# Parallel sum of a spectral filter and a spatial-shift MLP on one core: who normalises the first group, who splits w1's first quarter, and who takes one block's statistics

## The chip, the cores and the metric

The kernel runs on one core of a Trainium2 chip. The metric is the device time of one execution in microseconds. The engines are named as in the profile: PE (TensorE matmuls), PEld (TensorE weight loads), DVE (VectorE), ACT (ScalarE), POOL (GpSimd), SP (the engine that issues the transfers).

## The reference

With xn the layer norm of x (2048 tokens of 448 channels), the output is x + A(xn) + B(xn):

```python
# A: spectral filter
X = rfft2(xn) * (w_r + 1j * w_i);  a = irfft2(X)
# B: spatial-shift MLP
h  = gelu(layernorm(xn) @ w1)                    # 448 x 448
hs = shifted_quarters(h, (+1, -1, +2, -2)) @ w2  # 448 x 448
x1 = xn + hs
b  = x1 + gelu(layernorm(x1) @ w3) @ w4          # 448 x 1792, 1792 x 448
out = x + a + b
```

## The kernel before

The 2048 tokens are 16 blocks of 128, held as eight tiles `xt` of two blocks each. Four groups of four blocks are in `GRP`: group 0 is blocks 14, 15, 0, 1 and group 1 is blocks 2, 3, 4, 5. Every fp32 matrix product is made of three fp16 products: each operand is split into a high part (its fp16 rounding) and a low part (what is left), and high*high, high*low and low*high are added up in PSUM.

The change lies in the first 20 us, up to the first two groups' product with w1. The work there goes through these steps:

1. **Statistics and normalisation** (`norm1`, `stats`). For each block of a group DVE runs a statistics instruction (L306) and an aggregate (L307). Five short DVE instructions (L324 to L328) make scale and bias for the four blocks at once; then each block is scaled in place by the engine that the list `apply` names (L336 on DVE or POOL, L333 on ACT). `norm1` returns a function, `refine`, that adds ten small POOL instructions (L343 to L352) which sharpen the inverse root; their last result, `gsc`, is first wanted by the GELU.
2. **The scale of w1** (`squares`, `powers`). ACT adds up the squares of w1, DVE reduces them (L258), PE adds over the partitions with a matmul of ones into `pm` (L260), and DVE makes powers of two from that (L262 to L267): `s1`, the factor for w1, is written by L266.
3. **The split of w1** (`split_w`), in four row quarters t = 0 to 3. For t = 0 and 1 ACT writes the high part with the scale in it (L280) and DVE the low part (L281). For t = 2 and 3 POOL first scales the quarter in place (L276), ACT copies it to fp16 (L277), and POOL subtracts (L278).
4. **The transposition of x** (`T1`, `transpose_split`). For each of four column pieces PE transposes the group's four blocks (L389), ACT writes the high part (L393) and DVE the low part (L394). The fourth piece holds high and low part in one tile.
5. **The product with w1** (`w1_in`, L420), 11 matmuls for a block. For group 0 the first 24 run through quarters 0 and 1 for all four blocks, then quarters 2 and 3 follow for two of the blocks, 34 matmuls in all. Then PE transposes group 1, `T1(1)`, whose first transposition reads block 2.

Each engine works through its own list in order and waits at the head of it for semaphores. The order within a list is set by a scheduler that goes by priority and its own estimates, and by `behind(key)`, which lets an instruction be listed only after those recorded under that key; `pins` passes such keys to the statistics of `norm1`. ACT's outputs that nobody reads (the squares) go to a scratch tile, `xr`.

Of the kernel before, what the change touches and what calls it, by code (L numbers as in the profile page):

```python
# [125 lines left out]
def body(tc, nc, x, wf, w1, w2, w3, w4, c_g, c_n, c_small, out):  # L126
    V, A, P, T, SY = nc.vector, nc.scalar, nc.gpsimd, nc.tensor, nc.sync
# [31 lines left out]
    pc = pool("pc")  # L159
# [8 lines left out]
    def xb(b):  # L168
        return xt[b // 2][:, b % 2]
# [11 lines left out]
    xr = pw.tile([128, 904], F32, name="xr")  # L181
# [22 lines left out]
    w1s = stage("w1s", F, 0).rearrange("p (t n) -> p t n", t=4)  # L204
# [66 lines left out]
    def absmax(out_, in_):  # L271
        V.tensor_reduce(out=out_, in_=in_, axis=AX.X, op=ALU.max, apply_absolute_value=True)

    def split_w(hi, lo, src, s, low=None):
        if low is P:
            after["ps"] = (P.tensor_scalar(out=src, in0=src, scalar1=s, scalar2=0.0, op0=ALU.mult, op1=ALU.add).ins,)  # L276
            i = A.activation(out=hi, in_=src, func=AF.Copy)  # L277
            j = P.tensor_tensor(out=lo, in0=src, in1=hi, op=ALU.subtract)  # L278
            return i.ins, j.ins
        i = A.activation(out=hi, in_=src, func=AF.Copy, scale=s)  # L280
        j = V.scalar_tensor_tensor(out=lo, in0=src, scalar=s, in1=hi, op0=ALU.mult, op1=ALU.subtract)  # L281
        return i.ins, j.ins

# [13 lines left out]
        V.tensor_tensor(out=q, in0=q, in1=a, op=ALU.mult)  # L297
        V.scalar_tensor_tensor(out=r, in0=q, scalar=1.5 * 0.375, in1=w, op0=ALU.add, op1=ALU.mult)

    def stats(src, key, mv=None, pins=None):  # L300
        if mv is None:
            mv = pc.tile([128, 4, 2], F32, tag="mv", bufs=3, name=f"mv{key}")
        for i, s in enumerate(src):
            st = pc.tile([128, 6], F32, tag="st", bufs=4, name=f"st{key}_{i}")
            with behind(*pins[i]) if pins else contextlib.nullcontext():
                V.bn_stats(out=st, in_=s)  # L306
            V.bn_aggr(out=mv[:, i, :], in_=st)  # L307
        return mv
# [7 lines left out]
    vy = vyi.bitcast(F32)  # L316
    nma, nm1 = (pc.tile([128, NB], F32, name=f"nm{t}") for t in "a1")

    def norm1(g, apply, pins=None):

        bs, c = GRP[g], slice(4 * g, 4 * g + 4)
        mv, a, y, nm = mva[:, c], va[:, :, c], vy[:, :, c], nma[:, c]
        stats([xb(b) for b in bs], f"a{g}", mv, pins)
        V.tensor_scalar(out=a[:, 1], in0=mv[:, :, 1], scalar1=1.0 + EPS, scalar2=EPS * EPS, op0=ALU.mult, op1=ALU.add)  # L324
# [3 lines left out]
        i = V.scalar_tensor_tensor(out=nm, in0=mv[:, :, 0], scalar=-1.0, in1=y[:, 1], op0=ALU.mult, op1=ALU.mult)  # L328
        after["c", g] = (i.ins,)
        for k, b in enumerate(bs):  # L330
            y_, m_ = y[:, 1, k:k + 1], nm[:, k:k + 1]
            if apply[k] is A:
                i = A.activation(out=xb(b), in_=xb(b), func=AF.Identity, scale=y_, bias=m_)  # L333
                after["na", g] = (i.ins,)
            else:
                i = apply[k].tensor_scalar(out=xb(b), in0=xb(b), scalar1=y_, scalar2=m_, op0=ALU.mult, op1=ALU.add)  # L336
                after["n" if apply[k] is V else "np", g] = (i.ins,)

        q, z = (pc.tile([128, 2, 4], F32, tag=f"v{t}", bufs=2, name=f"v{t}{g}") for t in "qz")
        w, r = vw[:, :, c], vr[:, :, c]  # L340

        def refine():
            P.tensor_tensor(out=q, in0=y, in1=y, op=ALU.mult)  # L343
            P.tensor_tensor(out=q, in0=q, in1=a, op=ALU.mult)
# [3 lines left out]
            P.tensor_tensor(out=z, in0=w, in1=w, op=ALU.mult)  # L348
            P.tensor_tensor(out=z, in0=z, in1=q, op=ALU.mult)
            P.tensor_scalar(out=z, in0=z, scalar1=-0.5 * 0.375 ** 3, scalar2=1.5 * 0.375, op0=ALU.mult, op1=ALU.add)  # L350
            P.tensor_tensor(out=r, in0=z, in1=w, op=ALU.mult)
# [55 lines left out]
    w1p = p1.tile([128, 8, D], F16, name="w1p")  # L407
# [6 lines left out]
    def w1_in(g, units, ts, passes=range(3)):  # L414
        for p in passes:
            for t in ts:
                for i, pm in units:
                    wi, xi = ((0, 0), (0, 4), (4, 0))[p]
                    if t < 3 or p != 1:
                        m = T.matmul(pm[:, :D], xTs[g][:, xi + t, 128 * i:128 * i + 128], w1p[:, wi + t],  # L420
                                     start=t == 0 and p == 0, stop=t == 3 and p == 2)
        after["u"] = (m.ins,)
# [450 lines left out]
    for t in range(3):  # L873
        squares(m1[:, t:t + 1], w1s[:, t])
    squares(m1[:64, 3:4], w1s[:64, 3])
    n1 = [norm1(0, [P,V,P,V])]
    with behind("n", 0):
        s1, r1 = powers(m1, 4, "1", "mm")
    first = [bank("mm" if k < 2 else "sp", f"pw1_0{k}") for k in range(4)]
    for t in range(4):  # L880
        with behind("p1"):
            T1(0, [t])
        with behind("a0", t):
            after["w1", t] = split_w(w1p[:, t], w1p[:, 4 + t], w1s[:, t], s1, P if t > 1 else V)
# [12 lines left out]
    T1(1)  # L897
    with behind("T", "a1"):
        for unit in list(enumerate(first))[n:2]:
            w1_in(0, [unit], [2, 3])  # L900
    with behind("n", 1), behind("u"):
        s2, r2 = powers(m2, 1, "2", first[0][:, 448:512])
    with behind("p2"):
        for unit in list(enumerate(first))[2:]:
            w1_in(0, [unit], [2, 3])
# [31 lines left out]
    with behind("a2"):  # L937
        n1 = [norm1(3, [P, P, P, P])]
# [120 lines left out]
    for n in range(17):  # L1059
# [4 lines left out]
        if n:  # L1064
            b = bs[n - 1]
# [42 lines left out]
```

## Time and profile before

| what | value |
|---|---|
| median of 3 runs | 408.12 us (407.88 to 408.28) |
| the profiled execution's own time | 408.05 us |
| its span in the trace | 406.3 us |
| PE busy | 399.9 us, 98% of the span |
| DVE, ACT, POOL busy | 333.6 us (82%), 255.1 us (63%), 100.4 us (25%) |
| granted TensorE clock | 0.998 |

The profiled execution took 1.75 us more than its span, which is what lies before the first and behind the last instruction of the trace. In the profile's rows the first two numbers are the start of the row, in microseconds from the span's start, and its length; "x2" is the number of instructions in the row; the brackets give the idle time of the engine before it and what ended it.

### The profile page before, as it was taken

How to read it: one execution, taken by the hardware profiler on the slowest of the kernel's cores; microseconds unless marked ns; L12 is line 12 of the kernel's file. 1: busy time of each engine (PE TensorE's matmuls, PEld its weight loads, DVE VectorE, ACT ScalarE, POOL GpSimd, SP SyncE). 2: the span in 40 equal slices, each digit the busy share in tenths (PEclk: the TensorE clock that was granted, in tenths of full speed). 3: DMA queues.
4: the chain of work that ended last, by engine and by line, in shares of the span. 5: the costliest groups of instructions: out<-in, count | busy, mean ns of one | idle time of the engine just before them, and what ended most of it. 6: DMA issues, size and time to landing. Idle time of an engine off the chain costs nothing.

```text
span 406.3 us, 8732 instructions
## 1 busy us (share of the span) xinstructions
PE 399.9 (98%) x3391; PEld 297.2 (73%) x3391; DVE 333.6 (82%) x702; ACT 255.1 (63%) x433; POOL 100.4 (25%) x158
## 2 busy tenths in 40 slices
PE   8999999999999999999999999999999999999996
PEld 3555555865667877777878878777677779998995
DVE  5898799898947887988698888965999999965645
ACT  4788889874568857655698878853354544353431
POOL 6859910111146946500021111110000000000000
PEclk9999999999999999999999999999999999999999
DMA  8978975567489661637256556510011023100101
GB/s 280 389 272 160 249 152 138 122 121 163 95 225 266 234 191 46 219 95 185 72 144 164 162 142 161 139 27 2 24 69 70 24 90 92 47 2 2 45 2 45
DMA packets 54596, 52.07 MB, mean 128 GB/s; under 512 B 35678, under 2 KB 48542, under 8 KB 54556
## 3 DMA queue, kind: packets, MB, share of 16 engines
q1 hardware_dynamic: 54556, 51.53, 46.0%
q8 instruction: 26, 0.43, 0.4%
q14 instruction: 14, 0.11, 0.1%
HBM read 38.28 MB, written 3.67 MB: 103 GB/s over the span
## 4 chain that ended last, share of the span: by engine, by line
PE 87%; POOL 5%; DMA 2%; DVE 2%; ACT 2%; issue 1%; SPq 0%; POOLq 0%; ACTq 0%
PE pw L400 33%; PE acc L808 23%; PE pw L478 6%; PE side L778 4%; PE acc L778 3%; PE pu L667 3%; PE ps L567 3%; PE pe L688 2%; PE pp L622 2%; PE px L639 2%; PE py L709 2%; PE pw L420 2%; DMA w1s<-w 1%; POOL xt L336 1%; DMA h<-x2mem 1%
## 5 line engine op out<-in xcount | busy, mean ns | idle before, releaser
L400 PE MATMUL pw<-x2mem,w3p 128*128 128x256 f16 x1232 | 151.3, 273 | 0.0
L400 PEld LDWEIGHTS <-w3p 128*128 128x128 f16 x1232 | 118.9, 98 | 19.3
L808 PE MATMUL acc<-w4p,hf 128*128 128x448 f16 (+1 forms) x516 | 104.4, 348 | 0.0
L808 PEld LDWEIGHTS <-hf 128*128 128x128 f16 x516 | 50.1, 98 | 37.6
L726 ACT ACTIVATE pw<-pw,pe 128x512 f32<-128x512 f32 x42 | 27.4, 654 | 26.8 <-PE pw L400 26.6
L729 DVE SCALAR_TENSOR_TENSOR hf<-pw,h,hf 128x512 f16<-128x512 f32 x42 | 31.3, 746 | 12.9 <-ACT hf L728 12.7
L478 PE MATMUL pw<-w2p,h 128*128 128x448 f16 x176 | 35.8, 353 | 0.9 <-DMA h<-x2mem 0.9
L420 PE MATMUL pw<-w1p,xT 128*128 128x448 f16 x176 | 34.9, 352 | 0.1
L648 POOL TENSOR_TENSOR z<-te 128x450 f32<-128x450 f32 x16 | 15.7, 983 | 70.8 <-DVE te L646 65.9
L728 ACT ACTIVATE hf<-pw,h 128x512 f16<-128x512 f32 x42 | 28.9, 687 | 5.0 <-PE acc L808 4.0
L478 PEld LDWEIGHTS <-h 128*128 128x128 f16 x176 | 17.0, 98 | 17.0 <-DMA h<-x2mem 2.0
L744 ACT ACTIVATE hz<-g,h 128x896 f16<-128x896 f32 x14 | 14.6, 1044 | 23.1 <-DVE g L741 23.1
L420 PEld LDWEIGHTS <-xT 128*128 128x128 f16 x176 | 17.1, 99 | 16.1 <-DVE xT L394 0.4
L778 PEld LDWEIGHTS <-hz 128*128 128x128 f16 x294 | 28.3, 98 | 0.6
L629 ACT ACTIVATE pf<-pp 64x450 f16<-64x450 f32 x32 | 17.4, 544 | 12.5 <-DVE pf L630 9.7
L630 DVE TENSOR_TENSOR pf<-pp,pf 64x450 f16<-64x450 f32 x32 | 19.9, 622 | 5.1 <-ACT pf L629 4.7
L745 DVE SCALAR_TENSOR_TENSOR hz<-g,h,hz 128x896 f16<-128x896 f32 x14 | 16.1, 1148 | 6.8 <-ACT hz L744 6.8
L550 POOL TENSOR_TENSOR f<-xr 128x452 f32<-128x452 f32 x16 | 19.7, 1251 | 0.6
L558 DVE TENSOR_TENSOR xh<-f,xh 128x452 f16<-128x452 f32 x16 | 14.3, 916 | 5.7 <-ACT xh L557 5.7
L644 ACT ACTIVATE te<-px 64x450 f32<-64x450 f32 x32 | 17.3, 541 | 1.2 <-PE px L639 0.6
L738 ACT ACTIVATE g<-pw,pe 128x512 f32<-128x512 f32 x14 | 9.6, 683 | 11.3 <-PE pw L400 11.3
L547 POOL TENSOR_TENSOR xr<-xf 128x452 f32<-128x452 f32 x8 | 9.2, 1156 | 22.3 <-issue 16.4
(188 smaller groups left out, 705.7 us busy)
## 6 DMA issues: line engine op xcount, KB each, us to landing
wc<-wf SPq DMA_DIRECT2D x32, 225.0 KB, 3.7
wl<-wf SPq DMA_DIRECT2D x8, 450.0 KB, 4.3
xt<-x SPq DMA_DIRECT2D x8, 448.0 KB, 7.1
xf<-x SPq DMA_DIRECT2D x8, 448.0 KB, 4.6
loads<-x SPq DMA_DIRECT2D x7, 448.0 KB, 4.0
out<-xt SPq DMA_DIRECT2D x13, 224.0 KB, 1.9
w3raw<-w SPq DMA_DIRECT2D x3, 896.0 KB, 10.8
gn<-c_g SPq DMA_DIRECT2D x16, 128.0 KB, 3.0
```

Source lines behind the costliest of these rows:

```text
L400: T.matmul(ps_out, wp[:, wi + t, cols], xT[:, xi + t, tok], start=t == 0 and wi + xi == 0, stop=t == 3 and wi == 4)
L420: m = T.matmul(pm[:, :D], xTs[g][:, xi + t, 128 * i:128 * i + 128], w1p[:, wi + t], start=t == 0 and p == 0, stop=t == 3 and p == 2)
L478: T.matmul(pm[:, :D], h[:, k], w2p[:, w], start=n == 0, stop=n == 10)
L550: P.tensor_tensor(out=f[:, :, k:k + 2].rearrange("p b s d -> p s b d"), in0=u[:, :, 0], in1=u[:, :, 1], op=op)
L629: A.activation(out=hi, in_=src, func=AF.Copy)
L630: V.tensor_tensor(out=lo, in0=src, in1=hi, op=ALU.subtract)
L644: A.activation(out=e[64 * h:64 * h + 64], in_=px_[64 - 64 * h:128 - 64 * h, :2 * DF], func=AF.Copy)
L726: A.activation(out=pm, in_=pm, func=AF.Gelu_apprx_tanh, scale=r3)
L728: i = A.activation(out=h[:, 0], in_=pm, func=AF.Copy, scale=h3)
L729: j = V.scalar_tensor_tensor(out=h[:, 1], in0=pm, scalar=h3, in1=h[:, 0], op0=ALU.mult, op1=ALU.subtract)
L778: m = T.matmul(to, h[:, hi, 128 * blk:128 * blk + 128], b[wi], start=new and n == 0, stop=n == 2 and (last if blk in (2, 5, 3, 0) else end ...
L808: m = T.matmul(to, h[:, hi, o:o + 128], w4p[0][:, wi, f, r], start=first and f % 2 == 0 and n == 0, stop=end and f % 2 == 1 and n == 2, sk ...
```

## The change

Three things are moved, all in the steps above, and the two places in the text that follow from them.

- Group 0: the list of normalising engines goes from P, V, P, V to P, V, V, V. Block 0 moves from POOL to DVE.
- w1, quarter 0: `split_w` has a new argument `high`. For t = 0 POOL writes the scaled high part straight to fp16, in place of ACT; DVE still makes the low part.
- Group 1: `stats` has a new argument `on_a`. For block 5 ACT makes mean and variance with two activations that accumulate (the mean of x, then the squares of mean minus x) and a third that scales the sum; the DVE statistics and aggregate of that block go. The keys behind which the other three blocks' statistics are listed change, and the squares of w2 on ACT are listed behind the new third activation.

The matmuls of the last two blocks of group 0 with quarters 2 and 3 are now two pieces of text with the same key; a loop over nothing is gone.

```diff
-    def split_w(hi, lo, src, s, low=None):
+    def split_w(hi, lo, src, s, low=None, high=None):
         if low is P:
...
-        i = A.activation(out=hi, in_=src, func=AF.Copy, scale=s)
+        if high is P:
+            i = P.tensor_scalar(out=hi, in0=src, scalar1=s, scalar2=0.0, op0=ALU.mult, op1=ALU.add)
+        else:
+            i = A.activation(out=hi, in_=src, func=AF.Copy, scale=s)
         j = V.scalar_tensor_tensor(out=lo, in0=src, scalar=s, in1=hi, op0=ALU.mult, op1=ALU.subtract)
...
-    def stats(src, key, mv=None, pins=None):
+    def stats(src, key, mv=None, pins=None, on_a=None):
...
         for i, s in enumerate(src):
+            if i == on_a:
+
+                sq = pc.tile([128, 1], F32, tag="sq", bufs=2, name=f"sq{key}")
+                junk = xr.bitcast(F32)[:, :D]
+                with behind(*pins[i]):
+                    A.activation(out=junk, in_=s, func=AF.Copy, scale=1.0 / D, accum_out=mv[:, i, 0:1])
+                A.activation(out=junk, in_=s, func=AF.Square, scale=-1.0, bias=mv[:, i, 0:1], accum_out=sq)
+                u = A.activation(out=mv[:, i, 1:2], in_=sq, func=AF.Copy, scale=1.0 / D)
+                after["sq"] = (u.ins,)
+                continue
...
-    def norm1(g, apply, pins=None):
+    def norm1(g, apply, pins=None, on_a=None):
...
-    n1 = [norm1(0, [P,V,P,V])]
+    n1 = [norm1(0, [P, V, V, V])]
...
-            after["w1", t] = split_w(w1p[:, t], w1p[:, 4 + t], w1s[:, t], s1, P if t > 1 else V)
+            after["w1", t] = split_w(w1p[:, t], w1p[:, 4 + t], w1s[:, t], s1, (V, V, P, P)[t], P if t in (0,) else A)
...
-    n = 2
-    for unit in list(enumerate(first))[:n]:
-        w1_in(0, [unit], [2, 3])
+    units = list(enumerate(first))
+    w1_in(0, [units[0]], [2, 3])
+    w1_in(0, [units[1]], [2, 3])
...
-    n1.append(norm1(1, [P, V, A, V], [("r1",), ("a0", 0), ("w1", 0), ("w1", 1)]))
-    with behind("w1", 3):
+    n1.append(norm1(1, [P, V, A, V], [("e1",), ("w1", 0), ("w1", 1), ("a0", 3)], 3))
+    with behind("sq"):
         squares(m2, flat(w2s))
...
     with behind("p2"):
-        for unit in list(enumerate(first))[2:]:
-            w1_in(0, [unit], [2, 3])
+        w1_in(0, [units[2]], [2, 3])
+    with behind("p2"):
+        w1_in(0, [units[3]], [2, 3])
```

Lines from L281 on move down by 3 in the changed kernel, and those from L319 on by 13 (L336 becomes L349, L343 becomes L356).

The first place is DVE's list from the end of group 0's normalisation to w1's scale. `xt_83` holds blocks 14 and 15, `xt_76` blocks 0 and 1, `xt_77` blocks 2 and 3; `pt` and `pe` are the scale's small tiles. Before:

```order
L336 TENSOR_SCALAR xt_83<-xt_83,vy,nma 128x448
L336 TENSOR_SCALAR xt_76<-xt_76,vy,nma 128x448
L258 TENSOR_REDUCE pt_200<-m_167 128x1
L306 BN_STATS sta_0_298<-xt_77 128x6
L307 BN_AGGR mva<-sta_0_298 128x2
L262 TENSOR_SCALAR pt_200<-pm_202 128x1
L264 TENSOR_SCALAR pe_205<-pt_200 128x1
L266 TENSOR_SCALAR pe_205<-pe_205 128x1
```

And now:

```order
L349 TENSOR_SCALAR xt_83<-xt_83,vy,nma 128x448
L349 TENSOR_SCALAR xt_76<-xt_76,vy,nma 128x448 x2
L258 TENSOR_REDUCE pt_200<-m_167 128x1
L262 TENSOR_SCALAR pt_200<-pm_202 128x1
L264 TENSOR_SCALAR pe_205<-pt_200 128x1
L266 TENSOR_SCALAR pe_205<-pe_205 128x1
L267 TENSOR_SCALAR pe_205<-pe_205 128x1
L319 BN_STATS sta_0_298<-xt_77 128x6
```

One more normalisation stands ahead of L258, and block 2's statistics have moved from between L258 and L262 to behind the powers of two.

The second place is POOL's list from the normalisation of group 0 to that of group 1. `w1s` is w1 as loaded, `w1p` its split; `vq`, `vw`, `vz`, `vr` and `gsc` are the small tiles of `refine`. Before, from the second of its two normalisations of group 0:

```order
L336 TENSOR_SCALAR xt_76<-xt_76,vy,nma 128x448
L276 TENSOR_SCALAR w1s<-w1s,pe_205 128x448 x2
...
L348 TENSOR_TENSOR vz_199<-vw 128x8
L349 TENSOR_TENSOR vz_199<-vz_199,vq_198 128x8
L278 TENSOR_TENSOR w1p<-w1s,w1p 128x448
L350 TENSOR_SCALAR vz_199<-vz_199 128x8
L278 TENSOR_TENSOR w1p<-w1s,w1p 128x448
L351 TENSOR_TENSOR vr<-vz_199,vw 128x2x4
L352 TENSOR_SCALAR gsc<-vr,pe_205 128x4
L343 TENSOR_TENSOR vq_319<-vy 128x8
L336 TENSOR_SCALAR xt_77<-xt_77,vy,nma 128x448
```

And now:

```order
L281 TENSOR_SCALAR w1p<-w1s,pe_205 128x448
L276 TENSOR_SCALAR w1s<-w1s,pe_205 128x448 x2
...
L361 TENSOR_TENSOR vz_199<-vw 128x8
L278 TENSOR_TENSOR w1p<-w1s,w1p 128x448
L362 TENSOR_TENSOR vz_199<-vz_199,vq_198 128x8
L278 TENSOR_TENSOR w1p<-w1s,w1p 128x448
L363 TENSOR_SCALAR vz_199<-vz_199 128x8
L364 TENSOR_TENSOR vr<-vz_199,vw 128x2x4
L365 TENSOR_SCALAR gsc<-vr,pe_205 128x4
L356 TENSOR_TENSOR vq_320<-vy 128x8
L349 TENSOR_SCALAR xt_77<-xt_77,vy,nma 128x448
```

The high part of quarter 0 (L281) stands where block 0's normalisation stood, but it needs `s1`, which that did not; the two subtractions L278 stand one small step earlier each; and group 1's block 2 still comes last.

More of the change, by code (lines that the diff above doesn't have):

```diff
@@ L317, in body @@
     nma, nm1 = (pc.tile([128, NB], F32, name=f"nm{t}") for t in "a1")
-    def norm1(g, apply, pins=None):
+    def norm1(g, apply, pins=None, on_a=None):
         bs, c = GRP[g], slice(4 * g, 4 * g + 4)
         mv, a, y, nm = mva[:, c], va[:, :, c], vy[:, :, c], nma[:, c]
-        stats([xb(b) for b in bs], f"a{g}", mv, pins)
+        stats([xb(b) for b in bs], f"a{g}", mv, pins, on_a)
         V.tensor_scalar(out=a[:, 1], in0=mv[:, :, 1], scalar1=1.0 + EPS, scalar2=EPS * EPS, op0=ALU.mult, op1=ALU.add)
@@ L888, in body @@
         w1_in(0, list(enumerate(first)), [t])
-    n = 2
-    for unit in list(enumerate(first))[:n]:
-        w1_in(0, [unit], [2, 3])
+    units = list(enumerate(first))
+    w1_in(0, [units[0]], [2, 3])
+    w1_in(0, [units[1]], [2, 3])
     with behind("ps"):
         n1[0]()
-    n1.append(norm1(1, [P, V, A, V], [("r1",), ("a0", 0), ("w1", 0), ("w1", 1)]))
-    with behind("w1", 3):
+    n1.append(norm1(1, [P, V, A, V], [("e1",), ("w1", 0), ("w1", 1), ("a0", 3)], 3))
+    with behind("sq"):
         squares(m2, flat(w2s))
     T1(1)
-    with behind("T", "a1"):
-        for unit in list(enumerate(first))[n:2]:
-            w1_in(0, [unit], [2, 3])
     with behind("n", 1), behind("u"):
@@ L903, in body @@
     with behind("p2"):
-        for unit in list(enumerate(first))[2:]:
-            w1_in(0, [unit], [2, 3])
+        w1_in(0, [units[2]], [2, 3])
+    with behind("p2"):
+        w1_in(0, [units[3]], [2, 3])
     s12 = pc.tile([128, 4], F32, name="s12")
```

## The prediction

> **What bounds the kernel now.** I read the page first, then busy time by stretches, then the timelines of the first 35 us engine by engine.
>
> ```profile
> PE 399.9 (98%) x3391; PEld 297.2 (73%) x3391; DVE 333.6 (82%) x702; ACT 255.1 (63%) x433; POOL 100.4 (25%) x158
> ```
>
> Busy time by stretches (PE, PEld, DVE, ACT, POOL):
>
> ```profile
> 9.50:19.30 9.80, 9.04 (x53) 5.14 (x53) 9.16 (x26) 6.85 (x12) 8.17 (x18) 1.00 1.04 379
> 51.20:406.30 355.10, 351.80 (x3137) 271.69 (x3137) 293.33 (x577) 216.95 (x365) 60.72 (x68) 1.00 0.40 108
> ```
>
> PE sets the time: from 51.2 us on it is idle for 3.3 us in all, so whatever moves its arrival there moves the end. The change touches only what comes before 20 us. PE's timeline there:
>
> ```profile
> 9.54 0.38 PE L260 MATMUL pm<-pt,ones 128*128 128x1 f32 x2 [0.37 <-DVE pt L258]
> 9.79 2.00 PE L389 MATMUL pta<-ident,xt 128*128 128x128 f32 x16
> 11.72 6.92 PE L420 MATMUL pw<-w1p,xT 128*128 128x448 f16 x34
> 19.30 1.97 PE L389 MATMUL pta<-ident,xt 128*128 128x128 f32 x16 [0.66 <-POOL xt L336]
> 21.10 0.28 PE L260 MATMUL pw<-pt,ones 128*128 128x1 f32 x2
> 21.24 10.37 PE L420 MATMUL pw<-w1p,xT 128*128 128x448 f16 x54
> ```
>
> The reader is to see the gate at 19.30: PE has finished group 0's 34 matmuls at 18.64, idles 0.66 us, and is let go by POOL's normalisation of block 2. From there it runs without a gap past 31 us. 54 matmuls in 10.37 us are 0.19 us each; the 34 before would take 6.5 at that pace and took 6.92, so some 0.4 us of small stalls sit in them too. POOL's timeline up to the gate:
>
> ```profile
> 8.08 1.91 POOL L336 TENSOR_SCALAR xt<-xt,vy,nma 128x448 f32<-128x448 f32 x2 [2.57 <-DVE nma L328]
> 10.82 1.25 POOL L276 TENSOR_SCALAR w1s<-w1s,pe 128x448 f32<-128x448 f32 x2 [0.83 <-DMA w1s<-w]
> 12.04 0.20 POOL L343 TENSOR_TENSOR vq<-vy 128x8 f32<-128x8 f32 x1
> 12.32 0.70 POOL L344 TENSOR_TENSOR vq<-vq,va 128x8 f32<-128x8 f32 x1
> 14.07 0.73 POOL L348 TENSOR_TENSOR vz<-vw 128x8 f32<-128x8 f32 x1
> 14.88 0.20 POOL L349 TENSOR_TENSOR vz<-vz,vq 128x8 f32<-128x8 f32 x1
> 15.04 1.04 POOL L278 TENSOR_TENSOR w1p<-w1s,w1p 128x448 f16<-128x448 f32 x1
> 16.17 0.20 POOL L350 TENSOR_SCALAR vz<-vz 128x8 f32<-128x8 f32 x1
> 16.45 1.03 POOL L278 TENSOR_TENSOR w1p<-w1s,w1p 128x448 f16<-128x448 f32 x1
> 17.44 0.20 POOL L351 TENSOR_TENSOR vr<-vz,vw 128x8 f32<-128x8 f32 x1
> 18.07 0.20 POOL L343 TENSOR_TENSOR vq<-vy 128x8 f32<-128x8 f32 x1
> 18.30 0.94 POOL L336 TENSOR_SCALAR xt<-xt,vy,nma 128x448 f32<-128x448 f32 x1
> 19.21 0.33 POOL L344 TENSOR_TENSOR vq<-vq,va 128x8 f32<-128x8 f32 x1
> ```
>
> And DVE's:
>
> ```profile
> 7.92 0.93 DVE L336 TENSOR_SCALAR xt<-xt,vy,nma 128x448 f32<-128x448 f32 x2
> 9.33 0.16 DVE L258 TENSOR_REDUCE pt<-m 128x1 f32<-128x4 f32 x1 [0.47 <-ACT xr L253]
> 9.40 0.62 DVE L306 BATCH_NORM_STATS2 sta<-xt 128x6 f32<-128x448 f32 x1
> 10.06 0.18 DVE L307 BATCH_NORM_AGGREGATE mva<-sta 128x2 f32<-128x6 f32 x1
> 10.15 0.13 DVE L262 TENSOR_SCALAR pt<-pm 128x1 f32<-128x1 f32 x1
> 10.51 0.15 DVE L266 TENSOR_SCALAR pe<-pe 128x1 int32<-128x1 int32 x1
> 12.29 0.67 DVE L281 SCALAR_TENSOR_TENSOR w1p<-w1s,pe,w1p 128x448 f16<-128x448 f32 x1
> 14.09 0.66 DVE L281 SCALAR_TENSOR_TENSOR w1p<-w1s,pe,w1p 128x448 f16<-128x448 f32 x1
> 15.99 0.69 DVE L394 TENSOR_TENSOR xT<-pta,xT 64x512 f16<-64x512 f32 x1
> 16.92 0.58 DVE L324 TENSOR_SCALAR va<-mva 128x4 f32<-128x4 f32 x1
> 18.02 0.16 DVE L328 SCALAR_TENSOR_TENSOR nma<-mva,vy 128x4 f32<-128x4 f32 x1
> 18.22 1.26 DVE L336 TENSOR_SCALAR xt<-xt,vy,nma 128x448 f32<-128x448 f32 x2
> ```
>
> Two things stand here. From w1's scale (L266, done at 10.66) to the gate POOL has no pause of its own making: its list is as long as the way. And the two engines shut each other out: the small L344 and L348 take 0.70 and 0.73 us, until DVE's L281 beside them ends (12.96, 14.75), against 0.33 and 0.20 for their like; DVE's L324 takes 0.58, until POOL's L278 ends at 17.48.
>
> **The change part by part**, as what it does to the gate at 19.30.
>
> *Block 0 to DVE.* A third normalisation adds half of 0.93, so DVE is done at about 9.32; L258 waits for ACT until 9.33 anyway. Cost nothing, covered by the 0.47 us of idle time in L258's row; without that cover, 0.47. POOL's share leaves no gain: POOL waits for w1's scale until 10.82 either way.
>
> *Block 2's statistics out from between L258 and L262.* PE's `pm` is ready at 9.92 (9.54 + 0.38), L262 ran at 10.15 behind L306 and L307. It can go at 9.97: **-0.18**.
>
> *The high part of quarter 0 on POOL.* It enters ahead of everything else in POOL's list. The nearest row is L276, same shape and operation with one scalar: 1.25 for two, **+0.62**. It waits for L266, and behind it in the list stand the two scalings, `refine` and the gate itself. Bounds: 0.62 and the 0.95 of L336's 1.91 for two, which includes waits for DVE. PE's first matmul could then start near 11.55 instead of 11.72, ACT is relieved of 0.6 us, and the stalls in the 34 matmuls may go, since DVE reaches the last L394 (15.99) with two aggregates and one statistics fewer ahead of it. None of this counts while the gate behind is later: PE would be through at about 18.1 and wait longer.
>
> *The small steps of `refine`.* Each waits for the one before (12.04 to 12.32: 0.28). Now a subtraction stands between dependent ones. Before, L349 to L351 took 17.44 - 14.88 = 2.56. Now, from the same point less 0.08 for the wait that L278 doesn't have: 0.99 + 0.16 + 0.99 + 0.28 = 2.42 (0.99 is 16.45 to 17.44, 0.16 is 14.88 to 15.04). That is -0.22 at best; if ACT's copy or DVE get in the way, 0. I take **-0.15**.
>
> *Block 5's statistics on ACT.* DVE loses one 0.62 and one 0.18, none of it on POOL's path. ACT's three activations come behind the last high part of x and around the two copies L277, and end near 15.7 by the two ACT rows below (about 0.7 for an activation with its readout); DVE's L324 asks for them near 16.2, and behind it stand all four normalisations. Then ACT squares w2 (1.70 + 0.20), done near 17.6, ahead of its own normalisation at about 18.2. Cost nothing, with 0.5 us to spare; beyond that one for one.
>
> ```profile
> 8.63 0.58 ACT L253 ACTIVATE xr<-w1s 64x448 f16<-64x448 f32 x1
> 9.11 0.19 ACT L253 ACTIVATION_READ_ACCUMULATOR xr<-w1s 64x1 f32 x1
> 14.50 1.70 ACT L253 ACTIVATE xr<-w2s 128x1792 f16<-128x1792 f32 x1
> 16.09 0.20 ACT L253 ACTIVATION_READ_ACCUMULATOR xr<-w2s 128x1 f32 x1
> ```
>
> *The two engines meeting.* DVE's one-element `h1` (L886) now falls on POOL's new instruction: **+0.05** for the hand-over. And block 2's normalisation: POOL took 0.94 where half of L276's 1.25 is 0.62, so it lost about 0.3 to DVE's first L336 at 18.22. POOL now comes 0.3 us later, DVE's chain L324 to L328 hardly, since the second L278 now ends at about 17.8 and blocks it there. So DVE's normalisations run while POOL still has L351, L352 and L343 to do. DVE holds 0.47 each time; between nothing more than today and both, +0.65, I take **+0.15**.
>
> Sum: -0.18 + 0.62 - 0.15 + 0.05 + 0.15 = +0.49. The gate moves from 19.30 to about 19.8, and everything behind it by as much: group 1's first product ends on PE's pace, and the normalisation of group 2 and the transfers of h hang on that. The profiled execution took 408.05 (span 406.3 and 1.75 around it), 0.07 under the median of 408.12, so I set the shift on the median: **408.6 us**, 0.12% slower. A measurement of this kernel tells about 0.2%, 0.8 us, from no change; this lies inside.
>
> The row for DVE's pair at 7.92 is not stretched (0.93 for two) though POOL asked at 8.08: DVE kept POOL out until its second was nearly over. At 18.22 the pair took 1.26: POOL slipped in between. I count on the first for group 0's three. The Trainium skill (SBUF — State Buffer, "Who interferes with whom") says that the lock is held for one instruction and that whoever issues first gets it; by that rule POOL should take it at the first boundary, DVE's third would end 0.33 us later, and the sum would be 0.82.
>
> For elementwise work the Trainium skill (GPSIMD Engine Reference, section 3.1) speaks against POOL: it gives about 2.6 cycles an element for a sum of two inputs, at 1.2 GHz an estimate of 0.97 us for 448, and so a sum of 0.84 if the new instruction paid it too. The rows here agree for two inputs (L278, 1.04) and show 0.62 for one, which the new instruction has, so 0.62 stays.
>
> **The rivals.**
>
> *POOL's waits go (faster).* L344, L348 and L336 lose 0.37, 0.53 and 0.3 us to DVE. If DVE's L281 now meet long POOL instructions and wait themselves, up to 1.2 us vanishes: gate at 19.8 - 1.2 = 18.6, **407.4 us**. For it: DVE waited so at 16.92. Against: DVE's waiting makes L328 late, for which POOL waits too. PE itself would allow 18.0, 406.8 us.
>
> *Both of DVE's normalisations of group 1 go first (slower).* If DVE's chain is ready before POOL issues the second L343, POOL meets two holds with three instructions still to do: +0.65 in place of +0.15, gate at 20.3, **409.1 us**. It decides from the point where L328 ends before 18.0. For it: DVE has less to do. Against: L278's hold.
>
> *The hand-over inside group 0 (slower).* POOL takes its turn between DVE's first and second at about 8.4, L258 comes at 9.66, w1's scale 0.33 later: **408.9 us**. Against: the unstretched row.
>
> *Nothing reaches the end.* PE waits 0.36 us for a transfer of h at 33.7; if that absorbed the shift, **408.1 us**. Against: the transfer follows from the same products.
>
> ```profile
> 33.72 1.31 PE L478 MATMUL pw<-w2p,h 128*128 128x448 f16 x6 [0.36 <-DMA h<-x2mem]
> ```
>
> **How the numbers follow.** My forecast (408.2 to 409.0) 0.50, POOL's waits going 0.14, both normalisations first 0.18, the hand-over 0.10, nothing 0.08. Faster by over 0.2% (under 407.3) takes most of the first rival and a little for a gate set by PE: 0.12. Slower by over 0.2% (over 408.9): 0.16 of the second, half of the third and 0.05 of my own upper end: 0.26. Within: 0.62. The range runs from 407.4 (POOL's waits gone) to 409.3 (both normalisations first, and POOL's new instruction at 0.79, the middle of its bounds); beyond it lie about 0.08 below and 0.06 above.
>
> **What would show it.** Right: L262 at about 9.97; POOL's new L281 of 0.62 from 10.65; PE's first w1 matmul near 11.55, its 34 done by 18.2, then over 1 us idle until POOL's L349 lets it go near 19.8; no new gap behind. Wrong: the transpositions of group 1 starting before 19.2, or let go by another engine than POOL; the first L349 rows of DVE stretched; or PE's gap shifted behind 33 us.

## The result: 408.92 us against 408.12, slower by 0.2%

| | before | after |
|---|---|---|
| median of 11 runs each, same chip | 408.12 us (407.75 to 408.84) | 408.92 us (408.63 to 409.76) |
| ratio, 95% interval | | 1.0021 (1.0013 to 1.0029) |
| profiled execution | 408.05 us, span 406.3 | 409.76 us, span 407.9 |

The forecast was 408.6 in a range of 407.4 to 409.3, with 408.2 to 409.0 as the likeliest part: the sign and the range held, the sum was 0.3 us short, and the time grew for other reasons than the ones it was made of. The forecast had it that a change this small would not be told from none; the interval does tell it from none. The profiled execution of after is its slowest run; a second one (below) took 409.14. Both are used, and the rows are read from marks within an execution: VectorE's L258, the gate (PE's transposes of group 1) and PE's first product with w2.

The first line of after's page says that the bound is the same as before, and the windows (gate leg and steady part; PE, PEld, DVE, ACT, POOL) that PE idles 3.5 us in all behind the opening, where it was 3.3:

```profile
PE 400.2 (98%) x3391; PEld 297.5 (73%) x3391; DVE 332.9 (82%) x701; ACT 255.8 (63%) x437; POOL 100.1 (25%) x158
...
10.51:20.28 9.77, 8.62 (x52) 5.25 (x52) 8.39 (x25) 7.87 (x16) 8.01 (x18) 1.00 1.04 368
52.20:407.85 355.65, 352.15 (x3139) 271.77 (x3137) 293.26 (x578) 217.10 (x366) 61.39 (x68) 1.00 0.41 108
```

PE's timeline of after (start, duration, then engine, line, operands, count; in brackets the idle time before and who ended it):

```profile
10.51 0.38 PE L260 MATMUL pm<-pt,ones 128*128 128x1 f32 x2 [0.77 <-DVE pt L258]
10.76 1.95 PE L402 MATMUL pta<-ident,xt 128*128 128x128 f32 x16
12.54 6.59 PE L433 MATMUL pw<-w1p,xT 128*128 128x448 f16 x34
20.28 1.97 PE L402 MATMUL pta<-ident,xt 128*128 128x128 f32 x16 [1.15 <-POOL xt L349]
22.23 10.38 PE L433 MATMUL pw<-w1p,xT 128*128 128x448 f16 x54
35.16 1.31 PE L491 MATMUL pw<-w2p,h 128*128 128x448 f16 x6 [0.81 <-ACT x2mem L473]
```

Two things differ. PE waits 1.15 us at the gate where it waited 0.66, because its 34 matmuls begin 0.15 earlier after L258 and run without stalls (6.59 against 6.92). And a pause has grown behind the gate: 0.81 us ahead of L491, where it was 0.36, so that the way from the gate to w2 has grown from 14.42 us to 14.87. POOL's timeline of after, up to the gate:

```profile
8.08 1.21 POOL L349 TENSOR_SCALAR xt<-xt,vy,nma 128x448 f32<-128x448 f32 x1 [2.58 <-DVE nma L341]
11.57 0.64 POOL L281 TENSOR_SCALAR w1p<-w1s,pe 128x448 f16<-128x448 f32 x1 [2.28 <-DVE pe L267]
12.19 1.73 POOL L276 TENSOR_SCALAR w1s<-w1s,pe 128x448 f32<-128x448 f32 x2
13.89 0.20 POOL L356 TENSOR_TENSOR vq<-vy 128x8 f32<-128x8 f32 x1
14.16 0.20 POOL L357 TENSOR_TENSOR vq<-vq,va 128x8 f32<-128x8 f32 x1
14.81 0.38 POOL L359 TENSOR_TENSOR vw<-vw,vq 128x8 f32<-128x8 f32 x1
15.60 0.20 POOL L361 TENSOR_TENSOR vz<-vw 128x8 f32<-128x8 f32 x1
16.75 0.20 POOL L362 TENSOR_TENSOR vz<-vz,vq 128x8 f32<-128x8 f32 x1
18.90 0.37 POOL L356 TENSOR_TENSOR vq<-vy 128x8 f32<-128x8 f32 x1
19.27 0.96 POOL L349 TENSOR_SCALAR xt<-xt,vy,nma 128x448 f32<-128x448 f32 x1
```

The new L281 takes 0.64, as costed. But the small steps that had waited 0.70 and 0.73 for DVE (then L344, L348) now take 0.20 each (L357, L361), and from POOL's start on w1 to its normalisation it is 7.70 us (11.57 to 19.27) against 7.48 before (10.82 to 18.30): of the 0.64 put in, 0.22 is seen. DVE's timeline of after:

```profile
7.94 1.60 DVE L349 TENSOR_SCALAR xt<-xt,vy,nma 128x448 f32<-128x448 f32 x3
10.30 0.16 DVE L258 TENSOR_REDUCE pt<-m 128x1 f32<-128x4 f32 x1 [0.76 <-ACT xr L253]
10.93 0.16 DVE L262 TENSOR_SCALAR pt<-pm 128x1 f32<-128x1 f32 x1 [0.47 <-PE pm L260]
17.36 0.61 DVE L337 TENSOR_SCALAR va<-mva 128x4 f32<-128x4 f32 x1
18.50 0.16 DVE L341 SCALAR_TENSOR_TENSOR nma<-mva,vy 128x4 f32<-128x4 f32 x1
18.70 0.93 DVE L349 TENSOR_SCALAR xt<-xt,vy,nma 128x448 f32<-128x448 f32 x2
21.61 0.69 DVE L407 TENSOR_TENSOR xT<-pta,xT 128x512 f16<-128x512 f32 x1 [1.91 <-ACT xT L406]
22.21 0.80 DVE L475 SCALAR_TENSOR_TENSOR x2mem<-pw,h,x2mem 128x224 f16<-128x224 f32 x2
```

Three normalisations take 1.60 us, not 0.93 + 0.47 = 1.40. L262 runs 0.63 after L258, where it was 0.82. At the gate DVE's pair runs unbroken (0.93), and beside it POOL's L356 takes 0.37 and L349 0.96. And behind the gate DVE stands idle for 1.91 us until ACT's copy L406 of the first transposed piece; before, it had the low part of block 15's h to do in that time. That last row is the one that the forecast had no term for.

### The profile page after: what moved, and what is told of

It reads as the page before. It is cut to its first block, busy times and chain, and to the rows that moved or that the text cites. A ratio compares the mean times of both kernels' runs of the same rounds, so it can differ in the third digit from the quotient of the medians.

```text
span 407.9 us, 8735 instructions
## 1 busy us (share of the span) xinstructions
PE 400.2 (98%) x3391; PEld 297.5 (73%) x3391; DVE 332.9 (82%) x701; ACT 255.8 (63%) x437; POOL 100.1 (25%) x158
## 4 chain that ended last, share of the span: by engine, by line
PE 87%; POOL 4%; DVE 4%; DMA 3%; ACT 1%; issue 1%; SPq 0%; POOLq 0%; DVEq 0%; ACTq 0%
PE pw L413 33%; PE acc L821 23%; PE pw L491 6%; PE side L791 4%; PE acc L791 3%; PE ps L580 3%; PE pu L680 3%; PE pe L701 2%; PE pp L635 2%; PE px L652 2%; PE py L722 2%; PE pw L433 2%; DMA w1s<-w 1%; POOL xt L349 1%; DVE xT L407 1%; DMA h<-x2mem 1%
## 5 line engine op out<-in xcount | busy, mean ns | idle before, releaser
L491 PE MATMUL pw<-w2p,h 128*128 128x448 f16 x176 | 35.8, 353 | 1.3 <-ACT x2mem L473 0.8
L661 POOL TENSOR_TENSOR z<-te 128x450 f32<-128x450 f32 x16 | 15.7, 983 | 70.7 <-DVE te L659 65.8
L491 PEld LDWEIGHTS <-h 128*128 128x128 f16 x176 | 17.0, 98 | 17.5 <-DMA h<-x2mem 2.4
L570 ACT ACTIVATE xh<-f 128x452 f16<-128x452 f32 x16 | 8.7, 573 | 10.0 <-POOL f L563 8.3
```

What stands on the lines that cost most here:

```text
L491: T.matmul(pm[:, :D], h[:, k], w2p[:, w], start=n == 0, stop=n == 10)
```

## The experiments

Twelve runs follow, of eleven kernels (the changed one and only_v3 stand twice), each timed in five rounds beside the kernel before on the same chip. The runs were on three chips, so costs are taken from the ratios and not from the medians; a ratio's interval is in most of them about 0.4 us to each side. The table has medians and ratios, and from one profiled execution each: when L258 starts, how long it is from there to the gate, from the gate to the first product with w2, from there to PE's end, and what is left of that execution's own time. The five add up to it within 0.01.

| kernel | median us | ratio (95%) | L258 | to gate | to w2 | to PE's end | left |
|---|---|---|---|---|---|---|---|
| before | 408.12 | | 9.33 | 9.97 | 14.42 | 369.29 | 5.04 |
| none | 408.19 | 1.0000 (0.9989 to 1.0010) | 9.27 | 9.96 | 14.43 | 369.13 | 5.03 |
| after | 408.92 | 1.0021 (1.0013 to 1.0029) | 10.30 | 9.98 | 14.87 | 369.44 | 5.17 |
| after_again | 408.88 | 1.0022 (1.0013 to 1.0031) | 9.79 | 9.99 | 14.85 | 369.34 | 5.17 |
| without_v3 | 408.30 | 1.0005 (0.9996 to 1.0014) | 9.58 | 10.56 | 14.95 | 369.11 | 5.04 |
| without_hi | 408.92 | 1.0021 (1.0012 to 1.0031) | 9.62 | 9.86 | 14.86 | 369.38 | 5.08 |
| without_stat | 408.66 | 1.0014 (1.0005 to 1.0023) | 9.57 | 10.37 | 14.42 | 369.18 | 5.08 |
| only_v3 | 408.82 | 1.0022 (1.0013 to 1.0032) | 10.49 | 10.34 | 14.82 | 369.49 | 5.37 |
| only_v3_again | 408.77 | 1.0021 (1.0013 to 1.0030) | 9.57 | 9.98 | 14.45 | 369.43 | 5.34 |
| only_hi | 408.72 | 1.0017 (1.0008 to 1.0026) | 9.80 | 10.41 | 14.42 | 369.21 | 5.15 |
| only_stat | 408.74 | 1.0015 (1.0006 to 1.0023) | 9.13 | 10.67 | 14.87 | 369.22 | 5.19 |
| late_unit | 408.63 | 1.0012 (1.0003 to 1.0020) | 9.29 | 9.67 | 14.86 | 369.17 | 5.04 |
| unit_first | 409.95 | 1.0051 (1.0034 to 1.0067) | 9.50 | 9.96 | 14.62 | 370.03 | 5.06 |
| refine_late | 409.26 | 1.0033 (1.0020 to 1.0046) | 9.55 | 10.01 | 15.08 | 369.64 | 5.04 |

The column L258 has a part that no edit sets, since the data land at another time in each execution: ACT's first square of w1 starts at 6.27 in before, 7.35 in after, 7.20 in only_v3 and 6.06 to 6.72 in the others, and DVE's first normalisation at 7.92 in before, 8.26 in after_again, and 8.05 in none, without_stat and only_v3_again. These last three start alike, and are compared where L258 is the question: 9.57 with three normalisations on DVE, 9.27 with two. The column "to gate" moves as well: late_unit has the order of before in every list up to the gate, and took 9.67 where before and none took 9.97 and 9.96. So a difference of 0.3 us in that column, from one execution each, shows nothing unless a row explains it.

**The changed kernel again, and all three parts undone** (with the line numbers of after).

> The changed kernel once more, for a profile in which w1 lands as early as in the profile before (VectorE's L258 near 9.3 us; in the profile of the changed kernel it was 10.30, because w1's load landed 1 us later). Theory 1, the gate: GpSimd's list is longer by w1's quarter, L258 to the transposes of group 1 takes about 10.4 us instead of 9.97, and the rest is as before. Theory 2, the order behind the gate: L258 to the transposes stays near 10.0, and from there to the first w2 matmul it takes 14.9 us instead of 14.4. Both give a time near 408.9.

> The text of the change with all three moves taken back, every engine's order being that before the change. Both theories: 408.1, L258 to the transposes 9.97, from there to the first w2 matmul 14.4. It gives a second profile and shows how much w1's landing moves from run to run.

The cost came back (1.0022), and without the three parts there is none (1.0000): it belongs to the change. after_again against before, mark by mark: L258 +0.46, with DVE's normalisations starting 0.34 later; to the gate +0.02; to w2 +0.43; behind it +0.05; left +0.13.

**One part undone: group 0's normalisations.**

```
-    n1 = [norm1(0, [P, V, V, V])]
+    n1 = [norm1(0, [P, V, P, V])]
```

> The changed kernel with group 0 normalised as before (POOL twice, VectorE twice); the other two parts stay. Theory (the hand-over between VectorE's second and third normalisation costs 0.25 to 0.3 us ahead of L258, and the list behind the gate 0.44): L258 at about 9.3 us where w1's load lands early, 9.9 to 10.1 us from there to the gate, 14.86 us from the gate to the first product of w2, a time of about 408.6 us, ratio 1.0012 to 1.0016. Rival (POOL, busy 0.7 us longer with group 0, pushes its list to the gate back, and the gain ahead of L258 is lost there): 10.2 us or more from L258 to the gate and a ratio of 1.002 as for the changed kernel.

Measured: 1.0005, 0.6 us under the changed kernel. Of the three, this is the edit that costs most. The theory had 1.0012 to 1.0016, so it was too high. For the way to the gate its profile can't say why, since TensorE's clock was at half speed there for 3.4 us (last section). Behind the first product with w2 it can: to PE's end it took 0.23 us less than after_again, and 0.13 less is left (369.11 and 5.04 against 369.34 and 5.17). In after_again the 0.23 is one pause of PE ahead of a matmul of L580 at 145.3 us; without_v3 has no pause there. With the 0.30 ahead of L258 that makes 0.66, and 0.6 was measured.

**One part undone: quarter 0's high part.**

```
-(V, V, P, P)[t], P if t in (0,) else A)
+(V, V, P, P)[t], A)
```

> The changed kernel with w1's quarter 0 back on ScalarE (statistics of block 5 still on ScalarE, three normalisations on VectorE); the order behind the gate is that of the change. Theory 1: GpSimd's list is short again, about 408.0, L258 to the transposes 9.4 to 9.9. Theory 2: about 408.5, with 14.9 us from the transposes to the first w2 matmul.

Measured: 1.0021, the same time as with it; to the gate 9.86 against 9.99. Beside the other two edits, 0.64 us more work on POOL costs at most 0.13 us of the way to the gate, which is less than two executions of one order differ by, and nothing that the time shows.

**One part undone: block 5's statistics.**

```
-    n1.append(norm1(1, [P, V, A, V], [("e1",), ("w1", 0), ("w1", 1), ("a0", 3)], 3))
-    with behind("sq"):
+    n1.append(norm1(1, [P, V, A, V], [("r1",), ("a0", 0), ("w1", 0), ("w1", 1)]))
+    with behind("w1", 3):
```

> The changed kernel with block 5's statistics back on VectorE (GpSimd still writes w1's quarter 0, VectorE still normalises three blocks of group 0); behind the gate every engine's order is that before the change. Theory 1: the quarter on GpSimd is what costs, so about 408.7, with L258 to the transposes at 10.3 to 10.6. Theory 2: the order behind the gate came with the statistics, so about 408.2, with 14.4 us from the transposes to the first w2 matmul.

Measured: 1.0014. Beside the other two edits, the statistics on ACT buy 0.38 us ahead of the gate (9.99 against 10.37) and cost 0.43 behind it (14.85 against 14.42). What they buy is time on DVE; its timeline without them, one row of POOL's, and PE's:

```profile
14.36 1.41 DVE L284 SCALAR_TENSOR_TENSOR w1p<-w1s,pe,w1p 128x448 f16<-128x448 f32 x1
17.99 0.17 DVE L337 TENSOR_SCALAR va<-mva 128x4 f32<-128x4 f32 x1
18.68 0.16 DVE L341 SCALAR_TENSOR_TENSOR nma<-mva,vy 128x4 f32<-128x4 f32 x1
```

```profile
14.25 1.04 POOL L278 TENSOR_TENSOR w1p<-w1s,w1p 128x448 f16<-128x448 f32 x1
```

```profile
17.73 1.69 PE L433 MATMUL pw<-w1p,xT 128*128 128x448 f16 x8 [0.62 <-DVE xT L407]
19.94 1.97 PE L402 MATMUL pta<-ident,xt 128*128 128x128 f32 x16 [0.53 <-POOL xt L349]
```

L284 takes 1.41 us where it took 0.66 before, behind POOL's subtraction L278: the two lists meet there, DVE comes late to the statistics, PE stalls for 0.62, and at the gate POOL waits for DVE. The edit also moved that subtraction: the scheduler has put it behind L359, two small steps earlier than in after, where L278 starts at 15.76, with L284 done at 15.14.

```profile
18.73 0.20 POOL L356 TENSOR_TENSOR vq<-vy 128x8 f32<-128x8 f32 x1 [0.33 <-DVE vy L340]
```

**Each part alone.** Put into the kernel before: quarter 0's high part; the statistics; the normalisations, twice.

> The kernel before with w1's quarter 0 on GpSimd alone. If the quarter costs what it cost beside three normalisations: L258 to the transposes 10.35 to 10.45 instead of 9.97, then 14.42 to the first w2 matmul, 408.5. The prediction's term for it (0.62 less the reordering 0.15, plus meetings) gives 10.5 and 408.6; if GpSimd's waits swallow it, 9.97 and 408.1.

> The kernel before with block 5's statistics on ScalarE alone. Theory 2: the order behind the gate comes with it, so 14.85 us from the transposes to the first w2 matmul, against a gain of about 0.1 to 0.2 ahead of the gate (L258 to the transposes 9.8 to 9.9): 408.35 to 408.45. The prediction's term (0.18 gained, nothing lost): 407.9.

> The kernel before with block 0's normalisation on VectorE alone. Theory of the hand-over: GpSimd gets its turn between VectorE's second and third normalisation, the third takes 0.75 us instead of 0.51, L258 starts at 9.55 instead of 9.3 and everything behind it moves by 0.25: 408.35. The prediction's first term (nothing, covered by VectorE's idle time): 408.1.

Measured: 1.0017, 1.0015, 1.0022. Alone they cost 0.7, 0.6 and 0.9 us, together 0.9: they don't add. The high part alone has POOL's list in the order of without_stat, and the same long L284 and the same stall of PE (10.41 to the gate). The statistics alone cost time at the gate too (10.67): DVE's L337 meets the beginning of one of POOL's L278 (16.95, 1.04 long), takes 1.01 us, and POOL waits for DVE again:

```profile
17.00 1.01 DVE L337 TENSOR_SCALAR va<-mva 128x4 f32<-128x4 f32 x1
18.53 0.16 DVE L341 SCALAR_TENSOR_TENSOR nma<-mva,vy 128x4 f32<-128x4 f32 x1
```

In the profile of only_v3 TensorE's clock was at half speed for 3.4 us ahead of the gate (last section). The same kernel, profiled again without that:

> Only the choice of engines for group 0's normalisations, POOL once and VectorE three times, a second time, since the first profile of it had VectorE's L258 late (10.49 us) and TensorE's clock at 0.63. Theory (the cost is the hand-over inside group 0: VectorE's third normalisation about 0.75 us instead of 0.47, so L258 0.25 to 0.3 us later, and no other place): L258 at about 9.6 us where w1's load lands early, 9.97 us from there to the gate, 14.4 us from the gate to the first product of w2, and a time of about 408.45 us, ratio 1.0006 to 1.001. Rival (POOL, free earlier after one normalisation, changes how the engines meet ahead of the gate): 10.2 us or more from L258 to the gate, ratio 1.0015 to 1.0025.

The marks came as the theory said (9.57, 9.98, 14.45), the time as the rival said (1.0021). DVE's first normalisations and PE at the gate:

```profile
8.05 1.60 DVE L349 TENSOR_SCALAR xt<-xt,vy,nma 128x448 f32<-128x448 f32 x3
9.57 0.14 DVE L258 TENSOR_REDUCE pt<-m 128x1 f32<-128x4 f32 x1
```

```profile
19.56 1.97 PE L402 MATMUL pta<-ident,xt 128*128 128x128 f32 x16 [0.66 <-POOL xt L349]
34.01 1.31 PE L491 MATMUL pw<-w2p,h 128*128 128x448 f16 x6 [0.38 <-DMA h<-x2mem]
```

Its execution took 408.77, 0.95 more than that of none (407.82): 0.30 ahead of L258, 0.04 up to w2, 0.30 between w2 and PE's end, and 0.31 in what is left around PE's work. In the last two places no instruction was moved; against none DVE's list has one normalisation more and POOL's one less, and nothing else differs in either. So the place that the theory names is a third of what this edit costs alone. The rest can be found in the rows. The 0.30 is one pause of PE at 240 us, ahead of L652, and 19 us earlier POOL has lost as much on the way to it: its sixth L661 starts 0.43 us after the row of DVE that it waits for (L659, done at 221.25), where in none it starts 0.14 after it.

```profile
221.68 0.98 POOL L661 TENSOR_TENSOR z<-te 128x450 f32<-128x450 f32 x1 [3.93 <-DVE te L659]
240.41 0.74 PE L652 MATMUL px<-pf,gn 128*128 128x225 f16 x6 [0.18 <-DVE te L658]
```

From there ACT's and DVE's steps on the same data run 0.29 late until PE meets them. (From the start of the matmul ahead of it to its own, L652 takes 0.39 us here and 0.10 in none; the bracket counts from the modelled end.) The first profile of only_v3 has the same two rows. Of the 0.31, 0.22 lies in the barrier that ends the program: DVE's last DRAIN starts 0.46 us after the wait ahead of it ended, in none 0.09. The last section has what the two late starts have in common.

**The order behind the gate, alone.** The kernel before, with block 15's h listed behind the first transposed piece of group 1, as in the kernel after:

```
+            after["ev", key, t] = (i.ins,)
...
-        u = A.activation(out=h[0], in_=pv_, func=AF.Copy, scale=h1)
+        with behind("ev", "a1", 0) if (g, i) == (0, 1) else contextlib.nullcontext():
+            u = A.activation(out=h[0], in_=pv_, func=AF.Copy, scale=h1)
```

> The kernel before with one thing of the change's order alone: ScalarE writes the high part of group 1's first transposed piece ahead of the high part of block 15's product, and so VectorE the low part L394 ahead of the two L462 of that block (the two L462 of block 14 come side by side, as in the change). Nothing ahead of the gate differs. Theory 2, the order behind the gate: from the transposes of group 1 to the first w2 matmul 14.85 us instead of 14.42, time 408.5. Theory 1, everything comes from ahead of the gate: 14.4 us and 408.1.

From the gate to w2 it is 14.86, as in the kernels with the statistics on ACT (only_v3's 14.82 is from the execution with the low clock), and the time 1.0012. None of the change's own instructions is in this kernel. PE, and DVE behind the gate (18.97):

```profile
18.97 1.97 PE L402 MATMUL pta<-ident,xt 128*128 128x128 f32 x16 [0.60 <-POOL xt L349]
33.82 1.31 PE L493 MATMUL pw<-w2p,h 128*128 128x448 f16 x6 [0.79 <-ACT x2mem L475]
```

```profile
20.29 0.69 DVE L408 TENSOR_TENSOR xT<-pta,xT 128x512 f16<-128x512 f32 x1 [1.07 <-ACT xT L406]
20.90 0.80 DVE L477 SCALAR_TENSOR_TENSOR x2mem<-pw,h,x2mem 128x224 f16<-128x224 f32 x2
26.01 0.56 DVE L920 TENSOR_TENSOR s<-h,pe 128x1 f32<-128x1 f32 x1
26.56 0.80 DVE L477 SCALAR_TENSOR_TENSOR x2mem<-pw,h,x2mem 128x224 f16<-128x224 f32 x2
```

And DVE in the kernel none, whose order is that of before (gate at 19.23):

```profile
20.18 0.81 DVE L475 SCALAR_TENSOR_TENSOR x2mem<-pw,h,x2mem 128x224 f16<-128x224 f32 x2 [0.70 <-POOL vw L359]
20.90 0.68 DVE L407 TENSOR_TENSOR xT<-pta,xT 128x512 f16<-128x512 f32 x1
25.90 0.43 DVE L475 SCALAR_TENSOR_TENSOR x2mem<-pw,h,x2mem 128x224 f16<-128x224 f32 x1
```

With the old order DVE starts on h 0.95 us behind the gate, while PE still transposes; with the new one it idles until ACT's copy, 1.32 behind it, and comes to h 1.93 behind it. Later the one-element L920 stands ahead of block 14's h instead of inside it, and takes 0.56 beside POOL's scalings of w2 (0.22 before). So DVE has block 14's first part at 26.56 + 0.40, 7.99 behind the gate, against 25.90 + 0.43, 7.10 behind it. SyncE's L455 waits for just that; its queue in late_unit:

```profile
27.08 1.60 SPq L455 DMA_DIRECT2D x2mem<-x2mem  x2
30.80 1.34 SPq L485 DMA_TRANSPOSE h<-x2mem  x1
```

Behind it the transfer of h waits for DVE's next parts of h, and is issued 30.80 - 18.97 = 11.83 us behind the gate; in before it was 30.68 - 19.30 = 11.38. That is the 0.45.

**The old order put back into the changed kernel.** GELU and h of block 15 get their old place in the lists:

```
+            with behind(0, 1) if (key, t) == ("a1", 0) else contextlib.nullcontext():
...
+    kept, tc.cur_priority = tc.cur_priority, 247
+    w1_unit(0, 1, first[1])
+    tc.cur_priority = kept
...
```

> The changed kernel, with GELU and the two parts of h of block 15 put ahead of the first transposed piece of group 1 in ACT's and VectorE's lists again, as they stand in the kernel before; the order of some GELUs and transfers behind 25 us changes with it. Theory (0.44 us of the change's cost is this order, which the statistics on ACT bring with them): from the gate to the first product of w2 14.4 us instead of 14.86, and a time of about 408.45 us, ratio 1.0005 to 1.0012, if the later order costs nothing. Rival (the order is not what costs): 14.8 us there, and a ratio of 1.002 as for the changed kernel.

It gives 14.62, between the two, and loses more later: 0.7 us between w2 and PE's end, of which 0.5 is one new gap, and a time of 1.0051 with runs from 408.9 to 411.2. Moving the text also reordered GELUs and transfers further on, and that outweighs what it tests. No faster version came of it.

**Is it POOL's list?** The kernel before, with the small steps of group 0's reciprocal roots put behind the gate:

```
-    with behind("ps"):
-        n1[0]()
...
+    with behind("np", 1):
+        n1[0]()
```

> The kernel before, with POOL's reciprocal square roots of group 0 (the small steps, L339 to L351) put behind POOL's normalisation of group 1: POOL's list ahead of the gate loses them. It tests whether that list sets the gate. Theory (POOL's list is as long as the way): from L258 to the gate 9.2 to 9.4 us instead of 9.97, TensorE then being the next bound at 18.7; GELU of group 0, which needs the small steps, comes later, and if VectorE and POOL get the first transfer of h off as late as with the changed order, the gate to w2 takes 14.8 us or more and the time is 408.0 to 408.8 us. Rival (VectorE's chain or ACT sets the gate, POOL's list follows it): 9.9 us to the gate and a time that is the same or later.

The theory fell: 10.01 us to the gate, not 9.2 to 9.4, though POOL has ten instructions fewer to do (L343 to L352 of the kernel before). POOL now waits:

```profile
18.56 0.94 POOL L349 TENSOR_SCALAR xt<-xt,vy,nma 128x448 f32<-128x448 f32 x1 [2.24 <-DVE nma L341]
```

DVE's chain of statistics is ready as late as ever (L341 at 18.29, L258 at 9.55), but for another reason:

```profile
14.25 1.18 DVE L284 SCALAR_TENSOR_TENSOR w1p<-w1s,pe,w1p 128x448 f16<-128x448 f32 x1
17.60 0.17 DVE L337 TENSOR_SCALAR va<-mva 128x4 f32<-128x4 f32 x1
```

POOL's subtractions now start at 13.91 instead of 15.04, and DVE's second L284 waits for them, 0.52 us; the wait of the first short instruction at the end of the chain (0.58 in before) is gone. So two lists lead to the gate, POOL's and DVE's, and each is lengthened by the other. Without that meeting the gate would come some 0.5 us earlier (an estimate from the 1.18 and the 0.66); no run shows it, so it is not shown that DVE's list alone would hold the gate at 10 us. What it cost behind the gate (15.08) is h of group 0, which needs the roots.

## Why the prediction was right in size and not in its parts

- **The bound and the gate** held: POOL's normalisation of block 2 lets PE go in every profile here but two, where PE's own clock was low.
- **Block 0 to DVE, at nothing:** wrong. It was taken as covered by the 0.47 us in L258's row, and rested on DVE's unstretched pair. The third normalisation takes 0.75 us in every kernel that has it (0.51 alone): POOL's L349 gets its turn between the second and the third, L258 comes at 9.57 in place of 9.27, and the idle time that was to cover it is used up. It is the mechanism of the third rival, one boundary later than put there: +0.30 for its +0.33. The Trainium skill (SBUF — State Buffer, "Who interferes with whom") has it that whoever issues first gets the shared pair for the whole instruction; that POOL would then come in at the first boundary was the prediction's own reading, and the traces show the second boundary here, and the first in the pair at the gate in before (1.26 for two).
- **L262 without the statistics in its way, -0.18:** right. From L258 to the start of POOL's list it is 1.27 (after), 1.49 before.
- **The high part on POOL, +0.62:** the duration is right (0.64), and the 0.97 worked out from the Trainium skill (GPSIMD Engine Reference, section 3.1), which is for two inputs, is not what this form, with one, pays. Its weight was wrong. POOL's list was as long as the way, and in after it still is: L349 starts as L356 ends, 0.6 us after DVE's nma is ready (18.66). The step that failed is to add the 0.62 to that list as if the rest of it stood still. The rest holds POOL's waits for DVE, and they change with every shift (next point); and DVE's chain is the second list that leads to the gate. Alone, the high part costs 0.44 by the profile, since the subtractions in their new place make DVE wait in L284; with block 5's statistics gone from DVE, at most 0.13.
- **The small steps, -0.15, and the first rival:** the reordering gave -0.08 (from L278 at 15.76 to L364 at 18.32 it is 2.56, as from L349 to L351 before, without the 0.08 of wait ahead). The waits that the rival counted on did go (0.70 and 0.73 to 0.20 each) and were paid back in part by L276 (1.73 for 1.25): about -0.5 us more on POOL's list. It was given 0.14 as a way to a faster kernel; what it gained went into the +0.64.
- **Block 5's statistics on ACT, at nothing:** half right. ACT was in time, with about the spare time that was forecast: its normalisation waits 0.62 us for DVE's nma. But what DVE lost was on the way to the gate (9.99 against 10.37 in without_stat), and the statistics bring the new order behind the gate (last point).
- **The two engines meeting, +0.20:** 0.19 at the gate (L356 0.37 for 0.20, L349 0.96 for 0.94), in the second rival's order. The 0.05 of it for `h1` had no row behind it; L281 took 0.64, 0.02 over its price. DVE's pair did go first; the rival's +0.65 was too dear, since POOL had only L356 to do beside it.
- So the way to the gate is -0.22 + 0.64 - 0.08 - 0.5 + 0.19, about +0.03 (+0.02 between the marks), in place of **+0.49**, and L258 is +0.30 in place of nothing.
- **"Everything behind it by as much":** wrong, and the largest miss. The forecast looked at what sets the gate and not at what was listed behind it. The order changed there: +0.45 and +0.43 in the two profiles of after, and late_unit has it without any of the moved work. The row to mistrust stood in the profile before: PE's pause of 0.36 ahead of w2, where the transfer of h is already late, so that whatever delays h on DVE is paid in full.

That the sum came within 0.3 us is luck: 0.47 too much at the gate made up for part of the 0.73 ahead of L258 and behind the gate that had no term. The parts make 0.30 + 0.02 + 0.43 + 0.05 + 0.13 = 0.93, with the 0.30 from the executions that start alike; the medians differ by 0.8. The three normalisations are worth 0.6 to 0.9 us in the time, of which 0.30 lies ahead of L258; the rest lies at 145 or 240 us and behind PE's end, where no instruction was moved, at places found above and in the last section. What stays open is why an engine starts late there, and what brings the pause at 145 us.

## What to carry to other kernels

Where two engines that shut each other out lead to one gate, count both lists, and where they meet, before a cost is put on either: here ten instructions taken off one of them moved the gate by 0.04 us, since a long instruction of it then met the other list at a worse place, and 0.64 us put on it by at most 0.13 or by 0.44, as it met the other or not. Read the order of the lists behind the gate as carefully as ahead of it, first where the bound engine already waits for a transfer; a swap of two neighbours in ACT's list was worth half of this change's cost or more. And undo each part as well as doing it alone: the three cost 0.7, 0.6 and 0.9 us alone and 0.9 together.

## What the runs showed of the hardware that was not expected

*TensorE's clock can fall though TensorE was busy for half of the time.* In only_v3's first profile PE stood idle from 8.83 to 10.70, in that of without_v3 from 8.34 to 9.79. In only_v3 w1 landed late; in without_v3 the warm-up matmuls ahead of it had ended early (at 8.34, in the other profiles at 8.70 or later). A little later the granted clock (the column behind POOL's) was at half speed, for 3.4 us in both. Windows of without_v3:

```profile
8.34:9.79 1.45, 0.00 (x0) 0.00 (x0) 1.09 (x3) 1.18 (x4) 1.30 (x2) 1.00 1.02 394
10.78:14.19 3.41, 3.41 (x17) 2.69 (x15) 3.25 (x8) 2.95 (x6) 3.06 (x7) 0.50 1.05 295
```

and of only_v3:

```profile
11.77:15.19 3.42, 3.42 (x16) 2.33 (x15) 3.21 (x10) 3.42 (x8) 2.69 (x8) 0.50 1.06 346
```

After a pause of 1.16 (only_hi) it stayed at 1.00. In the 3.41 us ahead of the fall PE was busy for 1.95 us in without_v3 and for 1.55 in only_v3; in the stretch as far behind the clock's rise in only_hi (8.41 to 11.82) it was busy for 2.25, and the clock stayed. The Trainium skill (TensorE: Matmul & The Clock Gate, Part 1) has the clock fall after an idle window of about 3.4 us; here a pause of about half of that was enough in two executions of two.

*A short VectorE instruction waits for GpSimd like a long one.* L337 on 128x4 takes 0.17 alone, 0.61 behind one L278 and 1.01 in only_stat; L920 on 128x1 takes 0.56 beside the scalings of w2.

*An engine can start late at a fixed place in its list, whatever instruction stands there.* Here an engine's instructions are counted with its semaphore waits, which the rows leave out. In all eight profiles where the 197th of POOL is an L661, that L661 starts 0.43 to 0.45 us after the row of DVE that it waits for, and the other L661 of these profiles 0.08 to 0.15 after theirs. It is the fifth in after, after_again, without_stat, unit_first and refine_late, and the sixth, on the way to PE's pause at 240 us, in both profiles of only_v3 and in without_hi. In the other six the 197th is a wait, and no L661 is late. What is left of an execution behind PE's end goes by the length of DVE's list: 5.04 to 5.06 us with 830, 5.15 to 5.19 with 831, 5.03 to 5.08 with 832, and 5.34 and 5.37 with 833, where the 832nd is the DRAIN that starts late. So one instruction more or less on a list can cost up to 0.3 us elsewhere; why the engine is late there, no row shows.
